# Four edits to the order of work in a fused adaLN / memory-attention / gated-MLP kernel

## The chip, the cores and the metric

The kernel runs on one core of one Trainium2 chip. The metric is the device time in microseconds of one execution; lower is better. Before the change it is 258.24 us (median of 3 runs, 258.02 to 259.01). Beside the time each run gives the *span* (first to last instruction in the trace, some 1.7 to 2.5 us shorter than the time) and the mean clock that TensorE was granted, as a share of full speed.

TensorE's matmuls are called PE here, VectorE is DVE, ScalarE is ACT, GpSimd is POOL, and the queue of SyncE that issues transfers is SPq.

## The reference, cut to what matters

```python
# x: 2048 x 448, in 4 segments of 512 rows; 16 heads of 28; F = 1792
h = layernorm(x) * (1 + ca) + sa
for s in range(4):                                   # segments, in order
    p = softmax(q_s @ k_s^T * scale + causal_mask)
    a_dot = p @ v_s                                  # "PV"
    a_mem = (phi(q_s) @ M) / (phi(q_s) @ z + 1e-6)   # "memory read-out"
    out_s = g * a_mem + (1 - g) * a_dot
    M, z = M + phi(k_s)^T @ v_s, z + sum(phi(k_s))   # "memory product" dM
x = x + ga * (out @ wo)
h = layernorm(x) * (1 + cb) + sb                     # "LN2"
x = x + gb * ((sigmoid(h @ w_gate) * (h @ w_up)) @ w_down)
# phi(t) = t + 1 if t > 0 else exp(t), computed as min(exp(t), max(t, 0) + 1)
```

The segments form a chain through M: the read-out of segment 1 needs the first memory product. For the MLP of segment s ("gate/up jobs": two gate and two up products of 128x512 each) LN2 of the segment must be ready, transposed by DMA into the tile hT.

## The kernel before

The kernel is a hand-made schedule. Jobs of PE stand in a list (`fill`) and are dealt out between the attention steps; operations of DVE and POOL that PE does not need at once are put off with `later(ns, ...)` on a model clock that every job advances (`tick`). A smaller number puts an operation earlier in its engine's order. Nothing else is decided by it: every engine runs its instructions in the order given.

```python
def norm(self, i):                                   # LN2, one tile of 128 rows
    nc.vector.tensor_scalar(self.xn[:, i, 0:D], ..., op0=ALU.subtract, op1=ALU.mult)   # L277
    ...; eng.tensor_copy(self.xn[:, i, D:DP], ...)                                     # L281
def norm_t(self, i):
    self.norm(i)
    nc.sync.dma_start_transpose(self.h[:, :, i * P:(i + 1) * P], self.xn[:, i, :])     # L287

def phi(src, wait, tag, then=None):
    nc.scalar.activation(e[:], src, AF.Exp)
    def fin():                                       # the "minimum pair"
        nc.vector.tensor_scalar(r[:], src, 0.0, 1.0, op0=ALU.max, op1=ALU.add)         # L369
        nc.vector.tensor_tensor(e[:], e[:], r[:], ALU.min)                             # L370
    later(wait, fin, tag)

def mask(pT, kb):                                    # causal mask of the weights
    nc.gpsimd.affine_select(out=blk, in_=blk, compare_op=ALU.is_ge, ...)               # L437

# logits(s, hc, g):   if g == 0 and s > 0: pq_of[u] = phi(qT[:, hc, :], 5000, ("pq", u))
# wo_fin(s, t):       x_sb += pwo (L520); stats (L269, L270); rstd on POOL (L273, L274);
#                     later((3200, 2000, 2000, 1500)[s], lambda: ln.norm_t(t), ("ln2", s))

def gate_up2():                                      # second half of a gate/up job
    for fc, u, f, tt in zip(fcs, up, fs, tts):
        for k in range(3):
            nc.tensor.matmul(u[:, 0:L], lhsT=wu_sb[:, k, f], rhs=h[:, k, :], ...)
        nc.vector.scalar_tensor_tensor(ft[:], tt[:], 1.0, u[:, 0:L], ...)              # fT, L562

fill.extend(j2[8:] + m[0][1:] + j3[:2] + [(2000, prep_b2)] + j3[2:])   # m[0][1]: first dM

# main loop, per segment s, group of 4 heads hc, third g:
    logits(s, hc, g)
    if fill and fill[0][1] is gate_up2: fill.popleft()[1]()
    if prev[0] > 0 and g == 0: mem_read(*prev)
    if <g == 1, or g == 0 when behind> and prev in todo: pv(*prev)
    debt = run_fill(...)
```

PSUM has a pool of four banks for all products but the logits, so a product waits until a reader has freed a bank.

The softmax here doesn't subtract the row's maximum and nothing guards it: scores larger than these inputs give would overflow.

Of the kernel before, what the change touches and what calls it, by code (L numbers as in the profile page):

```python
# [17 lines left out]
def kernel(  # L18
# [17 lines left out]
    _, S, D = A_x.shape  # L36
# [30 lines left out]
    def m_f32(name):  # L67
        return ps_m.tile([P, 512], F32, tag="m", name=name)
# [7 lines left out]
    def later(ns, fn, tag):  # L76
        deferred.append((clock[0] + ns, len(deferred), fn, tag))

    def run_deferred(pick):
        while True:  # L80
            due = [d for d in deferred if pick(d)]
            if not due:
                return
            d = min(due, key=lambda d: d[:2])
            deferred.remove(d)
            d[2]()

    def tick(ns):
        clock[0] += ns
        run_deferred(lambda d: d[0] <= clock[0])  # L90
# [91 lines left out]
    for hs in range(4):  # L182
        nc.gpsimd.affine_select(out=bmask[:, :, hs, :], in_=bmask[:, :, hs, :], compare_op=ALU.is_ge,
                                fill=0.0, base=-HP * hs, pattern=[[0, NHC], [0, ME]], channel_multiplier=1)
        nc.gpsimd.affine_select(out=bmask[:, :, hs, :], in_=bmask[:, :, hs, :], compare_op=ALU.is_ge,
                                fill=0.0, base=HP * hs + Dh - 1, pattern=[[0, NHC], [0, ME]],
# [69 lines left out]
    MM, MV, TR = 216, 190, 60  # L256
# [106 lines left out]
    def phi(src, wait, tag, then=None):  # L363
        e = work.tile([P, L], BF16, tag="e", bufs=5, name="e")
        nc.scalar.activation(e[:], src, AF.Exp)

        def fin():
            r = work.tile([P, L], BF16, tag="r", bufs=2, name="r")
            nc.vector.tensor_scalar(r[:], src, 0.0, 1.0, op0=ALU.max, op1=ALU.add)  # L369
            nc.vector.tensor_tensor(e[:], e[:], r[:], ALU.min)  # L370
            if then:
                then(e)
        later(wait, fin, tag)
        return e
# [34 lines left out]
    pT_of, pq_of, ou_of, oT_of = {}, {}, {}, {}  # L409

    def logits(s, hc, g):
        u = (s, hc)
        qT, kT = qT_of[s], kT_of[s]
        if g == 0:
            pT_of[u] = pipe.tile([P, 4, PTW], BF16, tag="pT", bufs=2, name="pT")
        pT = pT_of[u]
        lg = ps_lg.tile([P, 4, 512], F32, tag="lg", name="lg")
        w0 = OFF[KB_GROUPS[g][0]]
        wid = 0
        for kb in KB_GROUPS[g]:  # L420
            nq = L - kb * P
            for hs in range(4):
                r = slice(HP * hs, HP * hs + Dh)
                nc.tensor.matmul(lg[:, hs, wid:wid + nq], lhsT=kT[r, hc, kb * P:(kb + 1) * P],  # L424
                                 rhs=qT[r, hc, kb * P:L], start=True, stop=True, tile_position=(HP * hs, 0))
            wid += nq
        nc.scalar.activation(pT[:, :, w0:w0 + wid], lg[:, :, 0:wid], AF.Exp, scale=scale)  # L427
        if g == 0 and s > 0:
            pq_of[u] = phi(qT[:, hc, :], 5000, ("pq", u))
        elif kq:  # L430
            kq.popleft()()
        for kb in KB_GROUPS[g]:
            later(2600, lambda kb=kb: mask(pT, kb), ("mask", u))
# [6 lines left out]
    def pv(s, hc):  # L440
        u = (s, hc)
        need(("mask", u))
        pT = pT_of.pop(u)
        vt = vt_all[s]
        acc = m_f32("acc")
        accv = acc[:].rearrange("p (t h e) -> p t h e", h=4, e=HP)
        for qb in range(TPS):
            for hs in range(4):
                for kb in range(qb + 1):
                    c0 = OFF[kb] + (qb - kb) * P  # L450
                    nc.tensor.matmul(accv[:, qb, hs, 0:ME], lhsT=pT[:, hs, c0:c0 + P],  # L451
                                     rhs=vt[:, kb, hc * 4 + hs, 0:ME], start=(kb == 0), stop=(kb == qb))
        ou = ou_bufs[(s * NHC + hc) % 2]
        ou_of[u] = ou
        ouv = ou[:].rearrange("p t h e -> p (t h) e")[:, :, 0:Dh]
        r1 = work.tile([P, TPS, 4], F32, tag="r1", bufs=2)
        nc.vector.tensor_tensor(r1[:], accv[:, :, :, Dh], cb(0, hc), ALU.mult)
        nc.vector.reciprocal(r1[:], r1[:])
        if s == 0:
            nc.vector.tensor_tensor(ouv, num(acc), bc(r1), ALU.mult)  # L460
            return
        t1 = work.tile([P, TPS * 4, Dh], BF16, tag="t1", bufs=1)
        nc.vector.tensor_tensor(t1[:], num(acc), bc(r1), ALU.mult)
        later(1400, lambda: nc.vector.tensor_tensor(ouv, t1[:], t2_of.pop(u)[:], ALU.add), ("ou", u))
# [52 lines left out]
    def wo_fin(s, t):  # L517
        pw = pw_of.pop(t)
        xt = x_sb[:, s * TPS + t, :]
        nc.vector.tensor_tensor(xt, pw[:, 0:D], xt, ALU.add)  # L520
        if t == 0:
            ln2_of[s] = LN([x_sb[:, s * TPS + i, :] for i in range(TPS)], ("2", s))
        ln = ln2_of[s]
        ln.stats(t)
        ln.rstd(t, t + 1)
        later((3200, 2000, 2000, 1500)[s], lambda: ln.norm_t(t), ("ln2", s))
        if t == TPS - 1:
            for kc in range(NK):
                later(6500 + 400 * kc, lambda kc=kc: ln.modulate(kc, 2), ("ln2", s))
# [3 lines left out]
    half = {}  # L533
# [17 lines left out]
            tts.append(tt)  # L551
        half[0] = (s, fcs, up, fs, tts)

    def gate_up2():
        s, fcs, up, fs, tts = half.pop(0)
        h = hT_of[("2", s)]
        for fc, u, f, tt in zip(fcs, up, fs, tts):
            for k in range(3):
                nc.tensor.matmul(u[:, 0:L], lhsT=wu_sb[:, k, f], rhs=h[:, k, :], start=False, stop=(k == 2))  # L559
            ft = pipe.tile([P, L], BF16, tag="fT", bufs=NFC + 2, name="fT")  # L560
            fT_of[(s, fc)] = ft
            nc.vector.scalar_tensor_tensor(ft[:], tt[:], 1.0, u[:, 0:L], op0=ALU.add, op1=ALU.mult)  # L562
# [45 lines left out]
    fill = deque()  # L608
# [101 lines left out]
    j0, j1, j2, j3 = [proj_jobs(s) for s in range(NSEG)]  # L710
# [14 lines left out]
    m = [mem_jobs(s) for s in range(3)]  # L725
# [34 lines left out]
                       + j1[:2] + m[0][0:1] + j1[2:4] + [ln1_start(3)] + j1[4:8], early_loads, 1))  # L760
    fill.extend(j1[8:] + [(1800, prep_b1)])
    fill.extend(j2[:8])
    fill.extend(j2[8:] + m[0][1:] + j3[:2] + [(2000, prep_b2)] + j3[2:])

    def cost(jobs):
        return sum(cst for cst, _ in jobs)
# [4 lines left out]
    todo = {(s, hc) for s in range(NSEG) for hc in range(NHC)}  # L771
    for s in range(NSEG):
        for hc in range(NHC):
            prev = (s, hc - 1) if hc else (s - 1, NHC - 1)
            for g in range(3):
                logits(s, hc, g)
                tick(450)
                if fill and fill[0][1] is gate_up2:
                    fill.popleft()[1]()
                    tick(6 * MM)  # L780
                    debt -= 6 * MM
                if prev[0] > 0 and g == 0:
                    mem_read(*prev)
                    tick(250)
                if prev[0] >= 0 and (g == 1 or g == 0 and s > 0 and (hc > 1 or s > 1) and pace[0] + debt <= 0) and prev in todo:
                    todo.remove(prev)
                    pv(*prev)
                    tick(1000)
                if prev[0] >= 0 and g == 2 and hc == 0:
                    otr(*prev)  # L790
                if (s, hc, g) in ((1, 0, 2), (2, 1, 0), (3, 1, 0)):
                    gj = gu_jobs(s - 1)
                    tail = list(fill)
                    print("left", s, cost(tail), len(tail))
                    fill.clear()
                    while tail and tail[0][1] is gate_up2:
                        fill.append(tail.pop(0))
                    if s == 1:
                        fill.extend(tail[:2])
                        tail = tail[2:]  # L800
                    for w in wo_jobs(s - 1):
                        fill.append(w)
                        if tail and s > 1:
                            fill.extend(tail[:2])
                            tail = tail[2:]
                    fill.extend((m[s][0:1] if s < 3 else []) + tail)
                    if s >= 2:
                        dj = down_jobs(s - 2)
                        if s == 2:
                            gj = gj[:8] + m[2][1:] + gj[8:]  # L810
                        fill.extend(dj + h2_jobs(s - 1) + gj)
                    else:
                        fill.extend(h2_jobs(s - 1) + gj[:8] + m[1][1:] + gj[8:])
                    pace[0] = (cost(fill) - KEEP[s] * GU) / (13, 12, 9)[s - 1]
                debt = run_fill(pace[0] + debt)
                if debt > 0:
                    print("dry", s, hc, g, debt)
                    debt = 0.0
                if g == 2 and hc > 0:
                    otr(*prev)  # L820
# [53 lines left out]
```

## Time and profile before

| | before |
|---|---|
| time, median | 258.24 us |
| span, granted clock | 255.8 us, 1.000 |
| first memory read-out starts (PE, mem L475) | 65.05 us |
| first gate product starts (PE, gps L542) | 82.16 us |
| from that product to the end | 173.6 us |

Lines of the timeline: start, duration, engine, line, operation, and in brackets the idle time in front with what ended it.

```profile
71.71 0.75 DVE L277 TENSOR_SCALAR xn<-x_sb,mv,rs 128x448 bf16<-128x448 bf16 x1
...
74.00 0.38 DVE L277 TENSOR_SCALAR xn<-x_sb,mv,rs 128x448 bf16<-128x448 bf16 x1
...
75.53 0.70 DVE L277 TENSOR_SCALAR xn<-x_sb,mv,rs 128x448 bf16<-128x448 bf16 x1
76.26 0.49 DVE L281 COPY xn<-xn 128x64 bf16<-128x64 bf16 x1
76.67 0.77 DVE L277 TENSOR_SCALAR xn<-x_sb,mv,rs 128x448 bf16<-128x448 bf16 x1
77.47 0.49 DVE L281 COPY xn<-xn 128x64 bf16<-128x64 bf16 x1
...
71.69 0.63 POOL L437 TENSOR_SCALAR_AFFINE_SELECT pT<-pT 128x512 bf16<-128x512 bf16 x1
...
75.28 2.65 POOL L437 TENSOR_SCALAR_AFFINE_SELECT pT<-pT 128x512 bf16<-128x512 bf16 x4
...
76.78 1.19 SPq L287 DMA_TRANSPOSE hT<-xn  x1
...
78.50 1.23 SPq L287 DMA_TRANSPOSE hT<-xn  x1
```

The same norm takes 0.38 us when POOL does no mask, and 0.70 to 0.77 us when it does: the first norm starts with a mask (71.69), the third and fourth lie in a burst of four (75.28 to 77.93). The small copy takes 0.18 or 0.49 us in the same way. The last line is the transpose of the fourth tile: its copy ended at 77.47 + 0.49 = 77.96, but it starts at 78.50. In front of it on the queue is the third tile's transpose, the line above it (76.78 to 77.97).

### The profile page before, as it was taken

To read this page: it belongs to the slowest core of one execution; us is meant where nothing else is said; L and a number is where in the kernel's file an instruction comes from. 1 tells how busy PE (TensorE), PEld (TensorE's weight loads), DVE (VectorE), ACT (ScalarE), POOL (GpSimd) and SP (SyncE) were. 2 spreads that over 40 slices of the span, in tenths; PEclk is the share of its full clock that TensorE was granted. 3 is DMA by queue.
4 is the path that set the end of the run, shared out by engine and by line. 5 is a ranking of instruction groups with operands and counts; after the bars stand their busy time and mean duration, and the time that the engine had idled before them with its cause. 6 is when DMAs were issued, how large, how long until landed. Compare 5 with 4: busy or idle time off the path is not lost.

```text
span 255.8 us, 5309 instructions
## 1 busy us (share of the span) xinstructions
PE 241.6 (94%) x2057; PEld 114.3 (45%) x2083; DVE 176.0 (69%) x419; ACT 139.4 (55%) x173; POOL 74.4 (29%) x140
## 2 busy tenths in 40 slices
PE   7999999978977999999999999999999999999994
PEld 2534544535533345355434355454343455333453
DVE  6878899856796886489878576885555486544422
ACT  0468879885896878585466847552753300133300
POOL 4368045315363221425502040471020023000000
PEclk9999999999999999999999999999999999999999
DMA  5999995691025212102432210113210015100011
GB/s 147 295 249 250 353 267 113 102 203 32 3 41 86 43 21 44 21 3 41 82 92 48 41 23 0 23 31 90 56 21 4 1 22 118 36 0 0 3 36 36
DMA packets 41168, 19.66 MB, mean 77 GB/s; under 512 B 30008, under 2 KB 40248, under 8 KB 41144
## 3 DMA queue, kind: packets, MB, share of 16 engines
q1 hardware_dynamic: 38408, 17.61, 31.6%
q10 hardware_dynamic: 2736, 1.72, 2.4%
q8 instruction: 16, 0.26, 0.5%
q14 instruction: 8, 0.07, 0.1%
HBM read 10.67 MB, written 1.84 MB: 49 GB/s over the span
## 4 chain that ended last, share of the span: by engine, by line
PE 59%; DVE 5%; DMA 2%; issue 1%; ACT 1%; DVEq 0%
PE dps L574 15%; PE ups L559 14%; PE gps L542 13%; PE gps L547 5%; PE pwo L510 4%; PE acc L451 4%; PE lg L424 3%; DMA hT<-xn 2%; PE mem L475 1%; PE ups L547 1%; DVE hT L291 1%; DVE fT L562 1%; DVE ot L576 1%; ACT pT L427 1%; DVE t L482 0%
## 5 line engine op out<-in xcount | busy, mean ns | idle before, releaser
L427 ACT ACTIVATE pT<-lg 128x2048 bf16<-128x2048 f32 (+1 forms) x48 | 76.8, 1600 | 26.1 <-PE lg L424 25.7
L562 DVE SCALAR_TENSOR_TENSOR fT<-tt,ups 128x512 bf16<-128x512 f32 x56 | 37.2, 687 | 38.7 <-PE ups L559 36.7
L550 ACT ACTIVATE tt<-gps 128x512 f32<-128x512 f32 x56 | 30.4, 595 | 56.1 <-PE gps L547 56.1
L437 POOL TENSOR_SCALAR_AFFINE_SELECT pT<-pT 128x512 bf16<-128x512 bf16 x64 | 40.8, 653 | 68.1 <-ACT pT L427 68.1
L574 PE MATMUL dps<-wd_sb,fT 128*128 128x448 bf16 (+1 forms) x238 | 43.9, 341 | 0.5 <-DVE ot L576 0.5
L542 PE MATMUL gps<-hT,wg_sb 128*128 128x512 bf16 x155 | 40.1, 379 | 1.9 <-DVE hT L291 1.1
L559 PE MATMUL ups<-hT,wu_sb 128*128 128x512 bf16 x165 | 40.6, 381 | 0.4 <-issue 0.3
L574 PEld LDWEIGHTS <-fT 128*128 128x128 bf16 x238 | 22.9, 98 | 19.4 <-issue 0.6
L559 PEld LDWEIGHTS <-wu_sb 128*128 128x128 bf16 x168 | 14.1, 98 | 22.3 <-issue 8.5
L542 PEld LDWEIGHTS <-wg_sb 128*128 128x128 bf16 x168 | 15.6, 98 | 18.7 <-DVE hT L291 1.5
L269 DVE BATCH_NORM_STATS2 st<-x_sb 128x6 f32<-128x448 bf16 x32 | 19.7, 616 | 0.5
L451 PEld LDWEIGHTS <-pT 128*128 128x128 bf16 x640 | 17.6, 96 | 3.9 <-issue 2.6
L451 PE MATMUL acc<-vt,pT 128*128 128x29 bf16 x640 | 18.6, 175 | 0.8 <-DVE t L482 0.5
L547 PE MATMUL ups<-hT,wgu_sb 64*128 64x512 bf16 x56 | 17.7, 382 | 1.1 <-ACT tt L550 0.5
L273 POOL TENSOR_SCALAR rs<-mv 128x1 f32<-128x1 f32 (+2 forms) x21 | 5.1, 244 | 46.1 <-DVE mv L270 45.0
L424 PE MATMUL lg<-qT,kT 28*128 28x512 bf16 (+3 forms) x256 | 17.3, 302 | 0.3 <-ACT pT L427 0.2
L547 PE MATMUL gps<-hT,wgu_sb 64*128 64x512 bf16 x56 | 17.0, 381 | 0.1
L576 DVE TENSOR_TENSOR ot<-dps,x_sb 128x448 bf16<-128x448 f32 (+1 forms) x17 | 9.9, 591 | 10.1 <-PE dps L574 10.1
L343 PE MATMUL pq<-hT,wq_sb 128*128 128x512 bf16 x58 | 16.3, 380 | 0.4 <-issue 0.2
L343 PE MATMUL pq<-hT,wk_sb 128*128 128x512 bf16 x61 | 16.3, 379 | 0.2
L277 DVE TENSOR_SCALAR xn<-x_sb,mv,rs 128x448 bf16<-128x448 bf16 x32 | 15.2, 496 | 1.7 <-POOL rs L274 1.5
L274 POOL TENSOR_TENSOR rs<-rs,mhalf 128x1 f32<-128x1 f32 (+2 forms) x21 | 14.3, 683 | 1.8
(101 smaller groups left out, 259.5 us busy)
## 6 DMA issues: line engine op xcount, KB each, us to landing
wm<-in_w_mod_dram SPq DMA_DIRECT2D x4, 392.0 KB, 5.9
x_sb<-in_A_x_dram SPq DMA_DIRECT2D x3, 448.0 KB, 5.0
wd_sb<-in_B_w_down_dram SPq DMA_DIRECT2D x3, 448.0 KB, 9.2
wg_sb<-in_B_w_gate_dram SPq DMA_DIRECT2D x3, 448.0 KB, 9.9
wu_sb<-in_B_w_up_dram SPq DMA_DIRECT2D x3, 448.0 KB, 11.0
out_dram<-ot SPq DMA_DIRECT2D x8, 112.0 KB, 1.8
out_dram<-ot ACTq DMA_DIRECT2D x7, 112.0 KB, 1.7
wm<-in_w_mod_dram SPq DMA_DIRECT2D x2, 196.0 KB
```

The lines of the kernel that those rows point to most:

```text
L269: nc.vector.bn_stats(st[:], self.srcs[i])
L343: nc.tensor.matmul(pq[:, 0:L], lhsT=head_cols(w_sb, k, hc), rhs=h[:, k, :], start=(k == 0), stop=(k == NK - 1))
L424: nc.tensor.matmul(lg[:, hs, wid:wid + nq], lhsT=kT[r, hc, kb * P:(kb + 1) * P], rhs=qT[r, hc, kb * P:L], start=True, stop=True, tile_posi ...
L427: nc.scalar.activation(pT[:, :, w0:w0 + wid], lg[:, :, 0:wid], AF.Exp, scale=scale)
L437: nc.gpsimd.affine_select(out=blk, in_=blk, compare_op=ALU.is_ge, fill=0.0, base=0, pattern=[[0, 4], [1, P]], channel_multiplier=-1)
L451: nc.tensor.matmul(accv[:, qb, hs, 0:ME], lhsT=pT[:, hs, c0:c0 + P], rhs=vt[:, kb, hc * 4 + hs, 0:ME], start=(kb == 0), stop=(kb == qb))
L542: nc.tensor.matmul(g[:, 0:L], lhsT=wg_sb[:, k, f], rhs=h[:, k, :], start=(k == 0), stop=False)
L547: nc.tensor.matmul(dst[:, 0:L], lhsT=wgu_sb[r:r + LW, f], rhs=h[r:r + LW, 3, :], start=first, stop=not first, tile_position=(r, 0))
L550: nc.scalar.activation(tt[:], g[:, 0:L], AF.Tanh, scale=0.5)
L559: nc.tensor.matmul(u[:, 0:L], lhsT=wu_sb[:, k, f], rhs=h[:, k, :], start=False, stop=(k == 2))
L562: nc.vector.scalar_tensor_tensor(ft[:], tt[:], 1.0, u[:, 0:L], op0=ALU.add, op1=ALU.mult)
L574: nc.tensor.matmul(dp[:, c], lhsT=fT_of[(s, fc)][:, t * P:(t + 1) * P], rhs=wd_sb[:, fc, c], start=(fc == 0), stop=(fc == NFC - 1))
```

## The change

Its intent: (1) the first memory product comes two projections later, when its transposed features have landed; (2) the minimum pairs of the queries' features come sooner on DVE, and (3) so do the LN2 norms of the first segment; (4) in a gate/up job whose second half falls between attention steps, PV or the memory read-out goes between the two up products.

```diff
@@ logits @@
-            pq_of[u] = phi(qT[:, hc, :], 5000, ("pq", u))
+            pq_of[u] = phi(qT[:, hc, :], 4300, ("pq", u))
@@ wo_fin @@
-        later((3200, 2000, 2000, 1500)[s], lambda: ln.norm_t(t), ("ln2", s))
+        later((2400, 2000, 2000, 1500)[s], lambda: ln.norm_t(t), ("ln2", s))
@@ gate_up2 @@
-    def gate_up2():
-        s, fcs, up, fs, tts = half.pop(0)
+    def gate_up2(n=2):
+        s, fcs, up, fs, tts = half[0]
         h = hT_of[("2", s)]
-        for fc, u, f, tt in zip(fcs, up, fs, tts):
+        for _ in range(min(n, len(up))):
+            fc, u, f, tt = fcs[-len(up)], up.pop(0), fs[-len(tts)], tts.pop(0)
@@ fill @@
-    fill.extend(j2[8:] + m[0][1:] + j3[:2] + [(2000, prep_b2)] + j3[2:])
+    fill.extend(j2[8:] + j3[:2] + m[0][1:] + [(2000, prep_b2)] + j3[2:])
@@ main loop @@
-                if fill and fill[0][1] is gate_up2:
-                    fill.popleft()[1]()
-                    tick(6 * MM)
+                split = bool(fill) and fill[0][1] is gate_up2
+                if split:
+                    fill.popleft()
+                    gate_up2(1)
+                    tick(3 * MM)
                     debt -= 6 * MM
                 if prev[0] > 0 and g == 0:
                     mem_read(*prev)
                     tick(250)
+                elif prev[0] >= 0 and g == 1 and prev in todo:
+                    todo.remove(prev)
+                    pv(*prev)
+                    tick(1000)
+                if split:
+                    gate_up2(1)
+                    tick(3 * MM)
```

Below, the edits have letters: **D** the later dM, **M** the sooner minima, **N** the sooner norms, **S** the split.

## The prediction

> **What bounds the kernel now.** I read the page first (busy shares), then the matmul engine's waits, then the timeline around each of its longest waits. From the page:
>
> ```profile
> PE 241.6 (94%) x2057; PEld 114.3 (45%) x2083; DVE 176.0 (69%) x419; ACT 139.4 (55%) x173; POOL 74.4 (29%) x140
> ```
>
> PE is the bound, and its instructions are the same before and after (4168 rows in both orders): only 14 us of 255.8 are not PE work, and part of them is start-up and end. The change can win only waits of PE. Those waits, from the view of PE's waits (us in total, times, longest):
>
> ```profile
> PE dM L397 <- DMA pk<-e: 1.9, 2, 1.2
> PE mem L475 <- DVE e L370: 1.6, 1, 1.6
> ...
> PE gps L542 <- DVE hT L291: 1.1, 1, 1.1
> ...
> PE ups L547 <- ACT tt L550: 0.5, 1, 0.5
> PE ups L547 <- DVE t L482: 0.4, 2, 0.3
> ```
>
> The first three are what the second to fourth part of the change aim at; the last two are what the split of the up products aims at. The timeline of PE shows where the first two lie and how far apart:
>
> ```profile
> 55.26 0.58 PE L397 MATMUL dM<-vt,pk 128*128 128x116 bf16 x8
> 56.45 0.38 PE L397 MATMUL dM<-vt,pk 128*128 128x116 bf16 x4 [0.62 <-DMA pk<-e]
> 58.09 0.39 PE L397 MATMUL dM<-vt,pk 128*128 128x116 bf16 x4 [1.25 <-DMA pk<-e]
> ...
> 75.66 0.39 PE L475 MATMUL mem<-rm,e 128*128 128x116 bf16 x4 [1.59 <-DVE e L370]
> ```
>
> The third lies at 82.16. Adding up start to start, the lost time is 2.2 us at the first (0.78 + 1.41 beyond the matmul's own step), 1.75 at the second, 1.27 at the third. They do not add, because of the busy times by stretch (start:end, length, then busy of PE, PEld, DVE, ACT, POOL):
>
> ```profile
> 66.00:78.00 12.00, 10.36 (x101) 5.02 (x99) 11.43 (x28) 10.39 (x13) 6.66 (x13) 1.00 0.12 23
> 78.00:82.20 4.20, 2.61 (x55) 1.49 (x54) 2.27 (x7) 3.40 (x5) 1.22 (x2) 1.00 0.48 97
> 82.20:125.00 42.80, 42.29 (x416) 19.92 (x421) 33.50 (x81) 30.04 (x34) 14.65 (x29) 1.00 0.22 35
> ```
>
> From 66 to 78 us VectorE is busy 11.43 of 12 us: there DVE is the bound, not PE. After 82.2 PE is nearly full (42.29 of 42.80).
>
> **What the Trainium skill says.** "Perfetto Trace Analysis", Tensor Engine Instruction: ACT, DVE and GpSimd are strict FIFO, PE reorders only weight loads. So an operation put earlier in DVE's order is paid by what then stands behind it; the trace agrees (the feature minima at 74.81 to 75.60 stand behind a norm and a copy that PE does not need). "PSUM — Partial Sum Buffer", Specifications: 8 banks of 512 fp32 values. The logits tile, 128x2048 f32 in the exp's row, is four of them, so four are left for gate, up, PV, memory and projections: each new product waits until a reader has freed one of four. The trace agrees (the ups waits on "tt" and "t"). "Perfetto Trace Analysis", DMA Instruction — HWDGE: the issue row does not hold the data movement; here a transpose's row is 1.2 us and the page has 2.4 us to landing.
>
> **Part 1, first memory product two projections later.** Before, dM is the 1st thing after the v projection, at 55.26, and its last transposed block lands at 58.06. In the changed order come first two projections (2 x 4 x 0.216 = 1.73 us), eight logits (0.33) and PV (1.0): dM starts at 55.26 + 3.06 = 58.3, just behind the landing. All 2.2 us of wait go. But its result has a deadline: the memory read-out at 65.05 needs rm. PE from 58.3: dM 0.86, modulation columns 1.2, then the logits of the third group, which wait for the exp of the second: ACT now does two evacuations first (57.0 + 0.53 + 0.59 + 0.59 = 58.7, exp 1.88) to 60.55; logits 0.22, two projections 1.73, logits 0.33: ready at 62.85. rm: DVE's order is PV's three operations (58.5 to 59.65), a weight scaling (0.61 to 1.06), minimum pair (0.28 + 0.42 alone, 0.72 + 0.42 beside GpSimd), copy of dM 0.64: 61.6 to 62.5; GpSimd's multiplication 1.07 to 1.38: 62.8 to 63.9, I take 63.15. So the read-out moves from 65.05 to about 63.15: **1.9 us won**, 0.3 of the 2.2 given to rm.
>
> **Parts 2 and 3, minima (5000 to 4300) and LN2 norms (3200 to 2400) sooner.** Both only reorder DVE between 66 and 78. New order after the third tile's statistics (70.7 on the old clock): norm+copy 0.9, PV's three 1.0, norm+copy 0.5 to 0.9, minimum pair 0.7: the features are ready near 74.0, where PE arrives at 74.0. The wait of 1.6 us is nearly gone. But behind it now stand the fourth tile's add and statistics (1.42), norm+copy 0.9, add 0.38, norm+copy 0.9: the last norm ends at 77.6 to 77.95 against 77.96 before. The set of DVE work ahead of the last norm is the same, so it ends no sooner, and transposes (2.4), modulation (0.65) and the first gate product follow it as before. Meanwhile PE, 1.6 us earlier, meets a new wait: PV needs the bank that the read-out's last operation (t, L482) frees, on DVE behind the last norm, at about 78.7, where PE is at 77.1. So **0 to 0.4 us, I take 0.1**: a wait turned into two others (PV for t, gate for hT).
>
> **Part 4, the split.** Seven jobs change: PV between the up products at old times 89, 133, 146, 184; read-out at 107, 141, 155. PE's work is equal. DVE's changes: fT of 0.68 us, then the reader of PV (1.1) or of the read-out (1.1), then the second fT, which frees its bank that much later. Per job, by the waits of the changed order:
> - 133: fT 134.2 to 134.9, PV's three to 136.2, then a minimum pair that the order puts ahead of the second fT, to 136.9, fT to 137.6. The second up of the next job wants that bank at 137.2: **+0.4 to 0.7**.
> - 89: same pattern, bank at 93.4 to 93.85 against 93.05, but the logits after it waited for an exp anyway (at 95.30, 0.3): +0.15.
> - 146: the wait of 0.38 at 151.57 for the memory sum goes, as that sum's copy comes 0.7 earlier: -0.38.
> - 141: the first up waits for t (144.75 against 144.19), the second is released by tanh at 145.26 as before: 0.
> - 107, 155, 184: same DVE work in a row, or the bank free in time (187.8 against 188.5): 0.
> Sum +0.3. The waits at 132.62 and 195.76 are at jobs not split and stay.
>
> **Sum.** -1.9 - 0.1 + 0.3 = -1.7 us from 258.24: 256.5. After 82 us PE is full, so what is won before it reaches the end; all weights were loaded by then.
>
> **Rivals.**
> (a) The three waits add: 2.2 + 1.75 + 1.27 = 5.2, less some: 253 to 254. For it: each wait is named by the diff. Against it: 11.43 of 12 us of DVE. It needs DVE operations to get shorter or norms to leave before 77.9. Norm rows range from 0.36 to 0.86 us, longer beside GpSimd, so a lucky interleaving could give another 1 us. 15%.
> (b) The split pays: with PV between, first fT and PV's readers spread better, all waits on ups (0.9 us on PE's list) go: 255.5. For it: that is its intent. Against it: the minimum pair ahead of the second fT. 20%.
> (c) The gain of part 1 is lost: the margin between dM's start (58.3) and the last landing (58.06) is small, and rm at 63.9 gives only 1.1 us; the split costs 0.7 twice: 257.7 to 258.3. 20%.
>
> **Range and chances.** The main line 256.0 to 257.2 has near half the weight; (a) and (b) set the low end at 254.8, (c) the high end at 257.8. Faster by over 2% would be under 253.1: only (a) in full, 0.05. Slower by 2% needs 5 us of new waits in a kernel whose PE order hardly changes: 0.01. The runs before spread 258.02 to 259.01, so about 0.5 us of this is noise.
>
> **What would show it.** Part 1 right: no wait of dM for pk, read-out of the first pair near 63.1 with a wait of 0 to 0.5 for rm. Parts 2 and 3 right: the wait of mem for e under 0.4, a new one of PV for t L482 over 1 us near 77, a wait of the first gate product for hT of 1 us or more still there, and that product near 80.2. Part 4 right: a new wait of an up product for fT near 135 (old 137). Wrong, if the first gate product starts under 79 (DVE was not the bound, rival a) or over 81.5 (rival c), or if the time from that product to the end differs from the 173.6 us of before by over 1 us.

## The result, and the profile after

| | before | after |
|---|---|---|
| time, median of 4 runs | 258.35 us (258.02 to 259.01) | 255.69 us (255.20 to 256.06) |
| span, granted clock of the profiled run | 255.8 us, 1.000 | 253.7 us, 1.000 |
| first memory read-out | 65.05 | 62.85 (-2.20) |
| second memory read-out | 75.66 | 71.74 (-3.92) |
| first gate product | 82.16 | 78.97 (-3.19) |
| from that product to the end | 173.6 us | 174.7 us (+1.1) |

The ratio is 0.9893 (95% interval 0.9864 to 0.9921): 1.1% faster. Ratios here are the mean time of one kernel's fast runs over that of the other's fast runs of the same rounds, so not quite the ratio of the medians quoted.

From the page of after, and from the view of PE's waits (us in total, times, longest). Line numbers of after beyond some 555 are one higher than those of before:

```profile
PE 242.8 (96%) x2083; PEld 113.9 (45%) x2083; DVE 173.1 (68%) x419; ACT 139.2 (55%) x173; POOL 73.9 (29%) x140
```

```profile
PE acc L451 <- POOL pT L437: 1.7, 1, 1.7
...
PE ups L547 <- DVE fT L563: 0.7, 2, 0.5
```

The waits of dM for pk (1.9 us) and of mem for e (1.6) are gone from the list. New is a wait of PV ("acc") of 1.7 us and one of the up products for fT. PE's busy time is up by 1.2 us though its work is the same: 26 of its records are missing from the trace of before (2057 against 2083).

The timeline of after, with the starts that answer to those of before, and the norms, masks and transposes of the same stretch:

```profile
62.85 0.39 PE L475 MATMUL mem<-rm,e 128*128 128x116 bf16 x4
...
71.74 0.39 PE L475 MATMUL mem<-rm,e 128*128 128x116 bf16 x4
...
76.43 1.15 PE L451 MATMUL acc<-vt,pT 128*128 128x29 bf16 x40 [1.70 <-POOL pT L437]
...
78.97 0.39 PE L542 MATMUL gps<-hT,wg_sb 128*128 128x512 bf16 x1 [0.62 <-ACT vt L357]
...
70.04 0.39 DVE L277 TENSOR_SCALAR xn<-x_sb,mv,rs 128x448 bf16<-128x448 bf16 x1
...
72.69 0.38 DVE L277 TENSOR_SCALAR xn<-x_sb,mv,rs 128x448 bf16<-128x448 bf16 x1
...
74.04 0.69 DVE L277 TENSOR_SCALAR xn<-x_sb,mv,rs 128x448 bf16<-128x448 bf16 x1 [0.46 <-POOL rs L274]
74.77 0.49 DVE L281 COPY xn<-xn 128x64 bf16<-128x64 bf16 x1
...
73.97 2.42 POOL L437 TENSOR_SCALAR_AFFINE_SELECT pT<-pT 128x512 bf16<-128x512 bf16 x4
...
75.29 1.20 SPq L287 DMA_TRANSPOSE hT<-xn  x1
```

Three of the four norms now lie ahead of POOL's burst. The norms together take 1.84 us instead of 2.60, their copies 1.03 instead of 1.34: 1.07 us less of DVE for the same instructions. And the last transpose starts 0.03 us after its copy (74.77 + 0.49 = 75.26) instead of 0.54. Measured from the first read-out, which takes part 1 out:

| from the first read-out (us) | before | after | difference |
|---|---|---|---|
| last copy ends | 12.91 | 12.41 | -0.50 |
| last transpose starts | 13.45 | 12.44 | -1.01 |
| first gate product starts | 17.11 | 16.12 | -0.99 |

So half of this gain is DVE ending sooner, half is the transpose's start on the queue. The busy times of that stretch, before and then after (start:end, length, then PE, PEld, DVE, ACT, POOL):

```profile
65.05:82.16 17.11, 13.88 (x163) 7.08 (x161) 14.12 (x36) 14.73 (x18) 7.88 (x15) 1.00 0.20 40
```

```profile
62.85:78.97 16.12, 13.80 (x165) 7.16 (x161) 13.22 (x36) 14.45 (x18) 9.33 (x18) 1.00 0.21 43
```

DVE does 36 instructions in both, in 13.22 us instead of 14.12. After the gate product the gain shrinks job by job (offset to before): -3.19 at the gate, -2.86 after the job of old time 89, -2.05 after the one of 133, -2.63 after the one of 146, -2.68 at 197, -2.10 at the end. The wait behind the largest step, in the timeline of after:

```profile
135.14 0.37 PE L547 MATMUL ups<-hT,wgu_sb 64*128 64x512 bf16 x1 [0.45 <-DVE fT L563]
```

### The profile page after: what moved, and what is told of

It reads as the page before. It is cut to its first block, busy times and chain, and to the rows that moved or that the text cites. A ratio compares the mean times of both kernels' runs of the same rounds, so it can differ in the third digit from the quotient of the medians.

```text
span 253.7 us, 5336 instructions
## 1 busy us (share of the span) xinstructions
PE 242.8 (96%) x2083; PEld 113.9 (45%) x2083; DVE 173.1 (68%) x419; ACT 139.2 (55%) x173; POOL 73.9 (29%) x140
## 3 DMA queue, kind: packets, MB, share of 16 engines
q10 hardware_dynamic: 2736, 1.72, 2.4%
HBM read 10.67 MB, written 1.84 MB: 49 GB/s over the span
## 4 chain that ended last, share of the span: by engine, by line
PE 47%; DVE 9%; DMA 2%; issue 2%; ACT 1%; POOL 1%; SPq 0%; POOLq 0%; DVEq 0%; ACTq 0%
PE ups L560 13%; PE gps L542 11%; PE dps L575 8%; PE gps L547 4%; PE acc L451 3%; PE lg L424 2%; PE pwo L510 2%; DMA hT<-xn 2%; DVE st L269 2%; DVE x_sb L520 2%; DVE fT L563 1%; PE ups L547 1%; DVE xn L277 1%; DVE ot L577 1%; DVE t L482 1%
## 5 line engine op out<-in xcount | busy, mean ns | idle before, releaser
L560 PE MATMUL ups<-hT,wu_sb 128*128 128x512 bf16 x168 | 42.2, 381 | 0.0
L542 PE MATMUL gps<-hT,wg_sb 128*128 128x512 bf16 x168 | 41.3, 379 | 0.9 <-ACT vt L357 0.6
L343 PE MATMUL pq<-hT,wq_sb 128*128 128x512 bf16 x64 | 17.0, 380 | 0.0
L277 DVE TENSOR_SCALAR xn<-x_sb,mv,rs 128x448 bf16<-128x448 bf16 x32 | 14.4, 471 | 2.1 <-POOL rs L274 2.0
```

The costliest lines, as they stand in the source:

```text
L343: nc.tensor.matmul(pq[:, 0:L], lhsT=head_cols(w_sb, k, hc), rhs=h[:, k, :], start=(k == 0), stop=(k == NK - 1))
L542: nc.tensor.matmul(g[:, 0:L], lhsT=wg_sb[:, k, f], rhs=h[:, k, :], start=(k == 0), stop=False)
```

## The experiments

Twelve kernels ran. The first four ran on one chip with 5 rounds each, the next four on another with one look each (for a single run the state is unknown), the last four on a third with 5 rounds. All twelve gave correct results. Times of the same kernel vary by about 1% with the granted clock (0.985 to 1.0 between executions), so the offsets in the profiled execution are the finer measure. The front of the kernel varies too, by transfers and the clock (up to 2 us), so each row is best read from the first read-out on. Offsets of starts against before, in us (the last two columns rest on spans rounded to 0.1 us, and are good to 0.1):

| kernel | edits | first read-out | first gate | third read-out (old 86.64) | old 129.8 | old 137.5 | old 153.2 | old 197.4 | end | read-out to end |
|---|---|---|---|---|---|---|---|---|---|---|
| after | D M N S | -2.20 | -3.19 | -3.19 | -2.86 | -2.05 | -2.63 | -2.68 | -2.1 | +0.1 |
| e9_whole | D M N S | -2.32 | -3.31 | -3.31 | -2.97 | -2.05 | -2.63 | -2.69 | -2.5 | -0.2 |
| e1_dm_only | D | -2.30 | -2.30 | -2.30 | -2.30 | -2.30 | -2.31 | -2.30 | -2.3 | 0.0 |
| e2_minima_norms | M N | +1.64 | +0.65 | +0.65 | +0.65 | +1.12 | +0.53 | +0.18 | +0.1 | -1.5 |
| e3_split | S | +2.00 | +2.00 | +2.00 | +2.00 | +1.96 | +1.38 | +1.39 | +2.0 | 0.0 |
| e4_no_split | D M N | -2.13 | -3.13 | -3.12 | -3.12 | -2.66 | -3.24 | -3.60 | -3.7 | -1.6 |
| e12_no_split | D M N | -0.96 | -1.95 | -1.95 | -1.95 | -0.97 | -1.56 | -1.91 | -1.9 | -0.9 |
| e6_dm_minima | D M | -1.55 | -1.90 | -1.89 | -1.89 | -1.41 | -1.99 | -2.34 | -2.4 | -0.9 |
| e7_dm_norms | D N | -2.39 | -4.03 | -3.78 | -3.77 | -3.77 | -3.78 | -3.78 | -3.8 | -1.4 |
| e10_dm_norms | D N | -2.02 | -3.67 | -3.41 | -3.41 | -3.38 | -3.38 | -3.38 | -3.3 | -1.3 |
| e11_late_minima | D N, M in part | -2.19 | -3.83 | -3.58 | -3.58 | -3.51 | -4.10 | -4.44 | -4.3 | -2.1 |
| e8_pair_behind | D N S, M but one | -2.14 | -3.13 | -2.07 | -1.74 | -1.72 | -2.30 | -2.35 | -2.4 | -0.3 |
| e5_busy_pool | D M N, POOL busy | -0.34 | -0.84 | -0.32 | -0.32 | +0.84 | +0.25 | -0.10 | -0.2 | +0.1 |

The theory to test, formed on the two traces: the norms got shorter because they moved out of POOL's burst. The first rival: the shortening belongs to part 1, which shifts PE against POOL; the second: the three early waits simply add.

**e1_dm_only.** Only D.

```diff
-    fill.extend(j2[8:] + m[0][1:] + j3[:2] + [(2000, prep_b2)] + j3[2:])
+    fill.extend(j2[8:] + j3[:2] + m[0][1:] + [(2000, prep_b2)] + j3[2:])
```

> Part 1 alone (first memory product two projections later; everything else as before). Theory (the wait of dM for the transposed features goes; what follows on VectorE keeps its old order and its old slow rows): first memory read-out at 62.9 instead of 65.05, first gate product of the kernel at 80.0 instead of 82.16 (2.2 sooner), four norm rows between 66 and 78 still sum to about 2.6 us, span 253.5, ratio to before 0.9915. Rival (the norms got shorter because part 1 shifted them against GpSimd, not because parts 2 and 3 reordered them): first gate product at 79.0 and norm rows summing to 1.8.

Measured: 255.45 us (255.17 to 256.69), ratio 0.9862 (0.9833 to 0.9892). The offset is -2.30 at the read-out and stays so to the end. The norms take 0.75, 0.38, 0.71, 0.77 us, as before. So part 1 is worth 2.2 to 2.3 us, all of it reaches the end, and the shorter norms are not its doing: the first rival falls.

**e2_minima_norms.** Only M and N.

```diff
-            pq_of[u] = phi(qT[:, hc, :], 5000, ("pq", u))
+            pq_of[u] = phi(qT[:, hc, :], 4300, ("pq", u))
-        later((3200, 2000, 2000, 1500)[s], ...)
+        later((2400, 2000, 2000, 1500)[s], ...)
```

> Parts 2 and 3 alone (minima 5000 to 4300, LN2 norms 3200 to 2400). Theory (the reordering takes three of four norms out of GpSimd's mask burst; PE's wait of mem for e only moves to PV): first memory read-out unchanged at 65.05, wait of mem for e gone, a new wait of PV of 1.5 us or more, norm rows sum to 1.8 instead of 2.6, first gate product at 81.1 (1.0 sooner), span 254.8, ratio 0.996. Rival a (the waits add: 1.75 + 1.27): first gate product at 79.2, ratio 0.988. Rival b (shortening belongs to part 1): first gate product at 82.1, ratio 1.000.

Measured: 259.12 us (257.64 to 259.79) beside 259.3 of before, ratio 0.9984 (0.9950 to 1.0018). The profiled execution came late to the first read-out (+1.64); from there to the gate product it gains 0.99, the same as in after, with norms of 0.38, 0.39, 0.38, 0.69 us. The time does not resolve it, the trace does. The additive rival is refuted. The later steps (+0.47 at 137.5, -0.59 at 153, -0.35 at 197) appear here without any split.

**e3_split.** Only S (the blocks gate_up2 and main loop of the diff).

> Part 4 alone (PV or read-out between the two up products). Theory (second fT stands behind a minimum pair and frees its bank late): first gate product unchanged at 82.16, then +0.3 at the job at 89, +0.4 to 0.8 at 133, 0 at 141, -0.4 to -0.6 at 146, end +0.3 to +0.6, ratio 1.001 to 1.002. Rival (the split is what pays, the waits of ups for t and tt go and no new one comes): -0.9 at the end, ratio 0.9965.

Measured: 259.14 us (259.03 to 259.82), ratio 1.0002 (0.9977 to 1.0027). My expectation failed at its main point: nothing is lost at 137.5 (+2.00 to +1.96). The split alone gains 0.58 at 153 and loses 0.66 in the last segment; at the job of 89, where the whole change loses 0.33, it loses nothing (+2.00 before and after it). So the loss at 137.5 in the whole change is not the split's alone.

**e4_no_split.** D, M and N, without S: the three one-line edits of the diff, with gate_up2 and the main loop as before.

> Parts 1 to 3 without part 4. Theory: first gate product at 78.97 as with the whole change, nothing lost at the jobs of 89 and 133 (0.33 and 0.83 there with the split), nothing won at 146 (0.59 with the split), so the product of the read-out near 153 is 3.2 sooner than before instead of 2.63, span 253.1 (0.5 under the whole change), ratio 0.9875 to 0.989. Rival (the split pays in the whole): span 254.2 or more, ratio 0.991 or more.

Measured: 255.43 us (253.86 to 256.02), ratio 0.9840 (0.9808 to 0.9872). The gate product is where it was in after (-3.13), the loss at 137.5 is there without the split (0.46, where I had expected none), the gain at 153 too (0.58), and 0.36 more at 197. From the read-out to the end this profiled execution is 1.6 to 1.7 us better than that of after.

**e5_busy_pool.** To test the contention by itself: as e4_no_split, with four useless masks on a scratch tile on POOL, in the place where the norms had come free of it.

```diff
+    def busy_pool():
+        for _ in range(4):
+            nc.gpsimd.affine_select(out=junk[:], in_=junk[:], compare_op=ALU.is_ge, fill=0.0, ...)
+        if s == 0 and t == 2:
+            later(1500, busy_pool, "busy")
```

> Parts 1 to 3 without the split (as e4), plus four GpSimd selects on a tile that nothing else reads, placed in GpSimd's order between the mask at 69.6 and the fourth tile's rsqrt, where GpSimd was idle from 70.2 to 72.8. Theory (VectorE's bf16 SBUF rows are longer while GpSimd runs, by contention and not by a dependence): the pad copy 0.18 to 0.49, the minimum pair 0.29 + 0.42 to 0.7 + 0.4 to 0.86, so the chain of norms ends 0.7 to 1.1 later, first gate product at 79.7 to 80.1 instead of 79.03. Rival (the length of those rows is by order or by a dependence, not by GpSimd being busy): rows as in e4, first gate product at 79.0.

Measured, one look: 257.38 us. Lines of its timeline:

```profile
72.01 2.97 POOL L507 TENSOR_SCALAR_AFFINE_SELECT junk<-junk 128x512 bf16<-128x512 bf16 x4
...
72.32 0.50 DVE L281 COPY xn<-xn 128x64 bf16<-128x64 bf16 x1
...
73.10 0.68 DVE L370 TENSOR_TENSOR e<-e,r 128x512 bf16<-128x512 bf16 x1
...
77.71 1.20 SPq L287 DMA_TRANSPOSE hT<-xn  x1
```

The copy beside the useless masks takes 0.50 us instead of 0.18, the minimum 0.68 instead of 0.42; the four useless masks take 2.97 us, where the burst of after took 2.42. Not every row beside the masks grows: L369, between these two, took 0.28 us as it does alone (72.73). From the first read-out the last copy ends at 12.97 us (12.39 in e4, 12.91 before): the gain on DVE is gone. I had expected the norms to end 0.7 to 1.1 us later than in e4; they end 0.58 later. And the gate product is still 0.50 sooner than before, relative to the read-out. The last line tells why: the transpose starts 0.03 us after its copy (77.19 + 0.49 = 77.68), as in after. So the experiment separates the two halves: POOL's work accounts for one half (0.5), the start on the queue for the other. I had sized the contention at the whole of it. What follows at the third read-out is put down to the clock of this execution, which was 0.63 from 80 to 84 us, and proves nothing. GpSimd's factor for the fourth tile was not held up by the useless masks: they ended at 74.98, and it started at 75.28, behind the statistics that it needs.

**e6_dm_minima** (D and M) and **e7_dm_norms** (D and N). Against e4_no_split:

```diff
 e6:
-        later((2400, 2000, 2000, 1500)[s], ...)
+        later((3200, 2000, 2000, 1500)[s], ...)
 e7:
-            pq_of[u] = phi(qT[:, hc, :], 4300, ("pq", u))
+            pq_of[u] = phi(qT[:, hc, :], 5000, ("pq", u))
```

> Part 1 and the sooner minima, norms as before. Theory: the wait of mem for e goes, but three norms still come after the fourth tile's statistics and meet the mask burst; norm rows sum to 2.2 or more, first gate product at 79.4 to 79.9 (part 1 alone: 79.86). Rival (the minima are what pays): first gate product at 79.0.

Measured, one look: 255.18 us. From the read-out to the gate product it gains 0.35: its last copy ends 0.68 sooner (12.23), but its last transpose starts 1.08 us after that copy, 0.52 behind the end of the third tile's transpose. As expected the read-out's wait goes and the norms' rows sum to 2.2 us (0.75, 0.38, 0.39, 0.69).

> Part 1 and the sooner norms, minima as before. Theory: three norms come ahead of the mask burst (rows sum to about 1.9), but the pair stands behind them, so mem waits for e by 1.9 or more and the work of PE behind it comes late: first gate product at 79.2 to 79.7, between part 1 alone (79.86) and all three (79.0). Rival (the norms alone give all): 79.0.

Measured, one look: 253.68 us, the gate product at 78.13. That is better than either theory had it, and better than all three parts together. Lines of its timeline:

```profile
73.44 0.39 PE L475 MATMUL mem<-rm,e 128*128 128x116 bf16 x4 [1.82 <-DVE e L370]
...
72.58 0.28 DVE L369 TENSOR_SCALAR r<-qT 128x512 bf16<-128x512 bf16 x1
72.96 0.43 DVE L370 TENSOR_TENSOR e<-e,r 128x512 bf16<-128x512 bf16 x1
73.30 0.71 DVE L277 TENSOR_SCALAR xn<-x_sb,mv,rs 128x448 bf16<-128x448 bf16 x1
```

The read-out's wait for e (1.82 us) is back, and costs nothing, because the gate product waits longer for the last norm. In after the minimum pair stands *ahead* of the fourth tile's add and statistics (the pair from 70.56, the add at 71.28), which pushes these back; then POOL computes the tile's factor, and DVE stands idle for 0.46 us before the last norm (the bracket at 74.04 above). Here the pair is done *while* POOL computes the factor, and the norm follows with no idle time. So removing the wait that the profile named cost 0.65 us at the gate product (1.64 gained from the read-out against 0.99), and 0.4 at the third read-out, since e7 meets a small wait for PV's reader just behind the gate product (1.39 against 0.99).

**e8_pair_behind.** The whole change, with the one minimum pair of (2,3) left at 5000, which puts it behind the second fT of the job at 133.

```diff
-            pq_of[u] = phi(qT[:, hc, :], 4300, ("pq", u))
+            pq_of[u] = phi(qT[:, hc, :], 5000 if u == (2, 3) else 4300, ("pq", u))
```

> The whole change, but the minima of one head group (segment 2, last group) due at 5000 again, which by the order puts the minimum pair behind the second fT of the split job at 133 instead of ahead of it; nothing else moves. Theory (the pair ahead of the second fT is what costs there): the wait of an up product for fT of 0.6 us near 135 is gone, the loss of 0.83 between the PV at 131 and the gate product behind it falls to 0.1 or less, span shorter by 0.7 to 0.8 than the whole change's. Rival (it is the split itself): the wait stays at 0.4 or more.

Measured, one look: 255.10 us. Nothing is lost at 137.5 (-1.74 to -1.72), against 0.81 in after. It does lose 1.06 between the gate and the third read-out, where after loses nothing; the busy times by stretch show a lower granted clock there (third figure from the right):

```profile
70.00:80.00 10.00, 7.68 (x83) 3.76 (x81) 7.90 (x23) 8.58 (x13) 4.94 (x9) 0.92 0.52 81
80.00:90.00 10.00, 9.75 (x94) 4.09 (x93) 7.18 (x20) 7.77 (x10) 1.34 (x3) 0.91 0.20 40
```

In after both stretches have 1.00. Cut finer, the clock is 0.50 to 0.57 from 79 to 82 us here, behind the wait of PV (1.7 us) and from that of the gate product on. I take that loss for the clock's, which no second run confirms; what the clock does to all these kernels is told below.

**The last four**, on one chip, 5 rounds each, before at 258.59 us (257.45 to 259.98). e9_whole is the whole diff again, e10_dm_norms is e7_dm_norms and e12_no_split is e4_no_split again; only e11_late_minima is new:

> The whole change again, beside three versions on one chip. Theory (first gate product 3.2 us sooner through parts 1 and the norms; split costs 0.3 at the job of old time 89 and 0.8 at that of 133, pays 0.6 at 146; a loss of 0.5 in the last segment was scatter of transfers): time 255.4 to 256.0 if before is 258.3, ratio 0.988 to 0.991, first gate product 79.0, and from the job of old time 195 to the end nothing lost. Rival: the loss of 0.5 in the tail belongs to the split: it shows again here (old 213.9: the add of the last output waits about 2 us for a transfer) and in none of the three unsplit kernels beside it.

> Part 1 and the sooner norms alone (no split, minima at 5000), now timed. In one look it had a span of 252.0 against 253.7 of the whole change. Theory (the sooner minima push the last norm of the first segment back by 0.9 us, the split loses 0.6): ratio to before 0.983 to 0.986, so 1.3 to 1.9 us faster than the whole change beside it; first gate product 78.1, a gain of 3.8 that stays constant to the end. Rival (all three are needed together, the look was luck of the clock): same as the whole change within 0.5 us.

```diff
-            pq_of[u] = phi(qT[:, hc, :], 5000, ("pq", u))
+            pq_of[u] = phi(qT[:, hc, :], 4300 if s > 1 and u != (2, 3) else 5000, ("pq", u))
```

(the edit of e11_late_minima against e10_dm_norms)

> As the one before, and minima at 4300 only in segments 2 and 3 without pair (2,3), where the runs showed a gain (0.58 at the job of old time 146, 0.36 at 195). Theory: first gate product 78.1 as there, no loss at old 133, gains of 0.58 and 0.36 later: span 251.1, 0.9 us faster than the one before, ratio 0.980 to 0.983. Rival: those two gains only take up a slack that the lateness of other kernels left, and one vanishes when the pairs of (2,0) to (2,2) alone move: gain 0 to 0.4.

> The change without its fourth part, again, beside the whole change on one chip. Theory (split costs, by the sum of the jobs: 0.33 at 89, 0.37 more at 133, nothing else): 0.7 us faster than the whole change, ratio 0.985 to 0.988; first gate product 79.0, loss of 0.46 at 133, 0 at 89. Rival (split is worth nothing either way, and the 1.6 us between the two spans before was scatter): same within 0.3 us.

| kernel | median us | range | ratio to before, 95% |
|---|---|---|---|
| e9_whole | 256.81 | 255.01 to 257.63 | 0.9910 (0.9871 to 0.9948) |
| e12_no_split | 255.03 | 254.18 to 255.58 | 0.9848 (0.9815 to 0.9880) |
| e10_dm_norms | 254.14 | 253.96 to 256.65 | 0.9840 (0.9798 to 0.9882) |
| e11_late_minima | 254.05 | 253.00 to 255.84 | 0.9817 (0.9777 to 0.9857) |

- e9_whole repeats the change: gate product at -3.31, the losses at the jobs of 89 (0.34) and 133 (0.92), the gain at 146 (0.58). In the last segment it loses 0.2, where the first profile of the change had lost 0.58. The line behind that loss, of after and then of e9_whole, is an output's addition in the last segment:

```profile
213.92 0.62 DVE L577 TENSOR_TENSOR ot<-dps,x_sb 128x448 bf16<-128x448 f32 x1 [1.97 <-DMA out_dram<-ot]
```

```profile
213.35 0.62 DVE L577 TENSOR_TENSOR ot<-dps,x_sb 128x448 bf16<-128x448 f32 x1 [1.39 <-PE dps L575]
```

The same kernel waited for an output transfer in one execution and for PE in the other: 0.4 us of that loss is scatter, not the change. Whose the rest is stays open: from 197 to the end the four profiles with the split lose 0.58, 0.21, 0.66 and, in e8, nothing; those without it at most 0.19 (e11).

- e12_no_split loses 0.98 at 133, more than the 0.46 expected, with no split at all. Its timeline there (DVE, POOL, then the PE wait that follows):

```profile
133.59 0.76 DVE L369 TENSOR_SCALAR r<-qT 128x512 bf16<-128x512 bf16 x1
134.39 0.73 DVE L370 TENSOR_TENSOR e<-e,r 128x512 bf16<-128x512 bf16 x1
...
133.57 1.27 POOL L437 TENSOR_SCALAR_AFFINE_SELECT pT<-pT 128x512 bf16<-128x512 bf16 x2 [2.62 <-ACT pT L427]
...
136.21 0.39 PE L547 MATMUL ups<-hT,wgu_sb 64*128 64x512 bf16 x1 [0.49 <-DVE t L463]
```

In before the same pair stands behind PV's three operations and takes 0.28 and 0.42 us (136.80 and 137.11). Sooner, it comes ahead of them, beside two masks, and takes 0.76 and 0.73; PV's bank is free that much later, and the up product waits for it. How much later hangs on hundredths of a microsecond. In e4, the same kernel with half the loss, the pair started 0.01 us before the first mask, and in e12 0.02 us after it. The lines of e4:

```profile
132.39 0.28 DVE L369 TENSOR_SCALAR r<-qT 128x512 bf16<-128x512 bf16 x1
132.40 1.53 POOL L437 TENSOR_SCALAR_AFFINE_SELECT pT<-pT 128x512 bf16<-128x512 bf16 x2 [2.62 <-ACT pT L427]
132.71 0.73 DVE L370 TENSOR_TENSOR e<-e,r 128x512 bf16<-128x512 bf16 x1
```

Whichever of the two started first kept its length: in e4 L369 took 0.28 us and the two masks 1.53, in e12 L369 took 0.76 and the masks 1.27. With the split (after), the same pair is ahead of the second fT, and the up product waits for that. So the loss at 133 comes from the sooner minimum of (2,3), whichever reader it delays, and not from the split; e3_split (no loss with the split) and e8_pair_behind (no loss with that one pair put back) say the same. The split may add to it: 0.81 and 0.92 with it, 0.46 to 1.16 without (e4 and e5), which these profiles do not tell apart.

- e10_dm_norms confirms e7: the gain made at the gate stays to the end, ratio 0.9840.
- e11_late_minima gains 0.59 at 153 and 0.34 at 197 as expected, and gives 0.1 to 0.2 back at the end. Its time is 0.6 us better than e10's by the ratios, within the noise of either; by the trace it is 0.8. Against the whole change it is 0.9% faster (0.9817 / 0.9910 = 0.9906), against before 1.8%. It is the best version found.

**The clock behind the waits.** The executions' mean clocks are not spread evenly: most lie near 1.0, 0.993 or 0.986. The traces show why. In e3_split the busy times by stretch of 1 us (same columns), during and after dM's waits for its transposed features:

```profile
56.00:57.00 1.00, 0.00 (x0) 0.00 (x0) 0.00 (x0) 1.00 (x3) 0.00 (x0) 1.00 1.37 168
57.00:58.00 1.00, 0.39 (x4) 0.22 (x4) 0.00 (x0) 0.43 (x2) 0.00 (x0) 1.00 1.81 166
58.00:59.00 1.00, 0.03 (x1) 0.03 (x2) 0.00 (x0) 0.00 (x0) 0.00 (x0) 1.00 0.62 128
59.00:60.00 1.00, 1.00 (x8) 0.49 (x8) 0.61 (x2) 0.00 (x0) 0.00 (x0) 0.98 0.00 0
60.00:61.00 1.00, 1.00 (x16) 0.32 (x15) 0.57 (x2) 0.62 (x2) 0.88 (x1) 0.50 0.07 16
61.00:62.00 1.00, 1.00 (x41) 1.00 (x39) 0.00 (x0) 1.00 (x1) 1.00 (x2) 0.50 0.00 0
62.00:63.00 1.00, 1.00 (x6) 0.32 (x3) 0.82 (x3) 0.82 (x1) 0.19 (x2) 0.50 0.00 0
63.00:64.00 1.00, 1.00 (x22) 0.66 (x20) 1.00 (x3) 0.32 (x1) 1.00 (x2) 0.82 0.00 0
```

From 56 to 59 us PE is busy 0.42 of 3 us, and from 60 to about 63.4 it runs at half clock. By the clock column one such dip is 0.02 + 3 x 0.50 + 0.18 = 1.70 us of full clock lost, 0.66% of the span: the step between 1.0 and 0.993. The Trainium skill has this: "TensorE: Matmul & The Clock Gate", section "What's actually happening", states that the clock is halved after an idle window of some 3.4 us and comes back after a busy one. The trace agrees in part: half clock, for 3.4 us, behind a stretch in which PE was nearly idle, but with a fully busy microsecond (59 to 60) between the two. I found dips behind dM's wait (e2, e3, both without D) and behind PV's and the gate's waits (e5, e8, both with the sooner minima in segment 1); e5 has one more near its start, at 11 us. Counting timed executions at 0.998 or more: 12 of 18 in e1, e10 and e11 (D, late minima in segment 1), 5 of 18 in e4, e9 and e12 (D, sooner minima there), 0 of 12 in e2 and e3 (without D). But before, also without D, had 2 of 11 on the chip of e1 to e4 and 6 of 11 on that of e9 to e12, and the first four runs of after had 1. So the count, over three chips, does not show that the edits decide where a dip falls. What the traces show is that a PE wait can be followed by a dip, and then costs more than its length. Part of what separates the times of e10 and e12 may lie there, and part of e1's gain: 3.6 us by the times, 2.3 by the trace.

## Why the prediction was right or wrong

The predicted 256.5 us (254.8 to 257.8) holds the measured 255.69. But the prediction named two signs that would make it wrong, and both appeared, by a hair: the gate product at 78.97 (under 79), and 1.1 us more from there to the end (over 1). Two errors, 1.2 us at the gate and 0.8 behind it, partly made up for each other; that the sum came so close is luck.

- **Part 1** (-1.9): right in mechanism, measured -2.2 to -2.3, unchanged to the end in e1_dm_only. The mis-sized term is the 0.3 given back to rm: POOL's multiplication ran from 61.64 for 1.06 us, ready before PE came.
- **Parts 2 and 3** (-0.1): this is the step that failed, measured -1.0. It was put as: "The set of DVE work ahead of the last norm is the same, so it ends no sooner, and transposes (2.4), modulation (0.65) and the first gate product follow it as before." Both halves are wrong. The same work became shorter, since three of the four norms left POOL's burst: that moved the last copy by 0.5 us. And the last transpose, which had started 0.54 us after its copy, started 0.03 us after it: another 0.5. The contention is shown by e5_busy_pool, which brought back the first half and not the second. So "11.43 of 12 us" was no floor: DVE's busy time there held rows that were longer only because of POOL (the four norms and copies took 3.94 us, and take 2.24 when all are alone). The prediction had the row lengths (0.36 to 0.86 us, "longer beside GpSimd") and left the point to rival (a) as luck. It could have been worked out: the Trainium skill, "SBUF — State Buffer", section "Who interferes with whom", says that a VectorE instruction in a two-port mode (which a bf16 copy or tensor_scalar between SBUF tiles can use) contends with GpSimd for a shared pair of ports, and so does one with two SBUF inputs when GpSimd reads SBUF; the rows of 0.38 against 0.69 to 0.77 agree.
- The new waits came as foretold in place but not in name. PV's wait was 1.70 us (foretold: over 1, for t L482). The trace names POOL's mask; t ended at 75.66 + 0.62 = 76.28 and the last mask at 76.39, so PV had both to wait for, and POOL came last. The gate product still waited (0.78 beyond its step), less than the foretold 1.
- **Part 4** (+0.3): by jobs, 89: +0.15 foretold, +0.33 measured; 133: +0.4 to 0.7, measured 0.81 to 0.92; 141, 155: 0 and 0; 146: -0.38, measured -0.58. Taken to 197 that is +0.3 against +0.5. The size at 133 was near, its owner was wrong: the pair "that the order puts ahead of the second fT" is there because of the *sooner minima*, and costs as much without the split. Missed was also that the sooner minima win 0.35 at 197, which no kernel that has the split as well shows. So the split beside the other edits costs 0.3 at 89 and that 0.35; from the read-out to the end e9 is 0.8 worse than e12, and by the times of the same rounds 1.6 us (0.9910 against 0.9848, whose intervals just overlap).
- The last segment: 0.58 lost in the first profile, 0.2 in the second, 0.66 in e3_split, none in e4_no_split and e8_pair_behind. No step of the prediction had it. Scatter of transfers is shown for 0.4 of it; that the split has a part in the rest is neither shown nor ruled out.
- **Rivals.** (a), that the waits add to 5.2 us, is refuted by e2_minima_norms (1.0 for the two); its aside, shorter norms, was half of the truth. (b), that the split pays, is refuted by e3_split (no time) and e9 against e12. (c), that part 1's gain is lost, is refuted by e1_dm_only.

- A reading that does not hold: the "4168 rows" of PE stand in no record. The traces have 2083 matmuls and 2083 weight loads, 4166 in all; the argument does not hang on it.

What stays open: why the fourth transpose starts 0.52 us behind the end of the third one's row where both norms end close together (before, e1, e6), and why the gain at 197 is gone with the split.

## What to carry to other kernels

Before moving an operation earlier on VectorE, look at what GpSimd does at the old and at the new place: the same set of instructions can be a microsecond shorter or longer, so "the same work ends at the same time" is not safe. Of several waits in a row, only the one that ends the stretch counts: here the minimum pair's wait looked like 1.6 us to win, and leaving it alone while the norms moved was the better kernel, since the pair then filled time in which VectorE waited for GpSimd. Take a change of several edits apart: this one held two that pay, one that pays in some places and costs in others, and one that, beside the others, only costs.

## What the Trainium skill lacked or had wrong

- "SBUF — State Buffer", "Who interferes with whom": it has the contention, which the prediction should have used, and says that the loser blocks for the whole of the other's instruction. The rows of before's burst agree, taken one by one: the masks end at 76.10, 76.73, 77.31 and 77.93, the two norms 0.13 us after such an end (76.23, 77.44), the two copies 0.02 to 0.03 us after one (76.75, 77.96). What it lacks is how much of a row counts. The two norms and two copies take 1.12 us alone, and a mask by itself 0.61 us (two in 1.22 at 132.11 us in e10, beside DVE operations that read PSUM), so whole rows in turns would need some 3.6 us; the burst took 2.65. GpSimd's rows are rough.
- "DMA: Bandwidth & Descriptors", "DMA Transpose (X-bar)": gives no spacing of transposes in one queue. Here a row takes 1.19 to 1.25 us, and the next starts 0.10 us after its end (third tile, e6) or 0.52 us after (fourth tile, in before, e1 and e6), though its data were ready.
- "TensorE: Matmul & The Clock Gate", "What's actually happening": speaks of an idle window, but PE was not idle. In the 3.4 us just before the dips it was busy for 1.0 us (e2), 1.4 (e3), 1.7 (e5, its later dip) and 1.9 (e8), and the clock still halved for 3.4 us, worth 1.70 us of the span in e3. The same page's "A second HAM failure mode: psum-queue depth-cycling" does report that short idle times between groups of matmuls make the clock swing, without saying how much idle time it takes; these traces give no threshold either, since 1.7 busy of 3.4 us (from 74.4 us in e12) passed without a dip.
